# State-space tables of a convolution layer: sums of the last X doubling as identity matmuls on TensorE with ScalarE evictions, Y extension in two wide products, seeds by ScalarE

**Chip, cores, metric.** One core of a Trainium2 chip. The metric is the device time of one execution in microseconds (us). Every ratio below is the mean time of one kernel's fast runs over that of the kernel before's fast runs of the same rounds on the same chip, so it is not quite the ratio of the medians quoted next to it. In the profile lines PE is TensorE, DVE VectorE, ACT ScalarE and SPq SyncE's DMA queue; L311 is a line of the kernel. To evict is to copy a result out of PSUM, where the matmuls here leave theirs.

## The reference

Four layers in a row with residuals: state-space convolution, local attention, and both again. The change touches only the building of the convolution kernel `K` for the first layer, which stays in use for the third.

```python
def _A_ref(u, A_re, A_im, B_re, B_im, C_re, C_im, log_dt, Dskip):   # u: [1, 2048, 512], N = 128 modes
    dt = jnp.exp(log_dt)[:, None]
    logdA = dt * (A_re + 1j * A_im);  dB = dt * Bc
    P = jnp.exp(logdA[:, :, None] * l[None, None, :])               # powers, l = 0..2047
    K = jnp.einsum("dn,dnl,dn->dl", Cc, P, dB).real
    ...                                                             # y = irfft(rfft(u) * rfft(K)), + u * Dskip
x = x + _A_ref(_layernorm(x), ...);  x = x + _B_ref(_layernorm(x), ...)   # twice
```

The kernel factors `l` into two indices: a table X of 32 powers and a table Y of 64 scaled powers, for 64 channels a round, and contracts them over the modes. Eight rounds make the 512 channels.

## The kernel before

The parts that matter, with cuts marked `...`. One round of the tables and their contraction:

```python
def double(self, T, m, lev, hc):                 # entries m..2m-1 from entries 0..m-1 by a complex multiply
    for e0 in range(0, m, HALF):                 # HALF = 8
        ta = self.wk.tile(..., tag="ta");  tb = self.wk.tile(..., tag="tb")       # single scratch tiles
        nc.vector.tensor_tensor(v(ta), src, self.mult(self.MA, lev, hc, mm), ALU.mult)
        nc.vector.tensor_tensor(v(tb), src, self.mult(self.MB, lev, hc, mm), ALU.mult)
        nc.vector.tensor_tensor(T[..., m + e0:m + e0 + mm, :], ta[...], tb[:, ::-1, ...], ALU.add)

def half(hc, between=None):
    Xt, Y, Y2 = T.build(hc)                      # X has two buffers, Y and Y2 one each
    ...
    T.x_part(Xt, hc)                             # seed and four doublings, VectorE
    T.y_base(Y, hc)                              # seed and four doublings, VectorE
    T.y_products(Y, Y2, hc)                      # six products of 2048 elements, VectorE
    r = between() if between is not None else None     # a piece of the convolution
    with tc.high_priority():
        T.contract(Xt, Y, Y2, hc)                # 256 small matmuls into psk, one ScalarE eviction to KTq
    return r
```

The piece of the convolution between two tables has two stages of matmuls, with DMA transposes in between. It is `u_fft` in even rounds (the input) and `k_fft` in odd ones (the kernel `K`). A round on the page is counted from 1 to 8.

```python
def s1(self, rhs_j, n, drow=None):               # first stage
    for jq in range(NJ // 4):                    # four groups of eight matmuls
        ps = self.pst([128, 2, 16, 32])
        ...                                      # 8 matmuls (TensorE)
        self.evac("z", Z[..., jq * 32:(jq + 1) * 32], ps[...])     # one Z eviction (ScalarE), 1.0 us
    return Z

def s2(self, Z, cs, dsts, what):                 # second stage
    zts = self.turns(Z, cs)                      # DMA transposes zt <- Z: they need all four evictions of Z
    ...                                          # 16 matmuls from zt, evictions to xc, W or Kt
```

The scheduler puts the instructions of each engine into one fixed order when the kernel is built. That order is not the order of the source. `high_priority` moves the contraction forward in it.

## Time and profile before

| | before | where it is read |
|---|---|---|
| time | 530.74 us (528.93 to 532.49), 3 runs | times |
| VectorE busy, table stage 62 to 227 us | 153 of 165 us | table of windows (in the prediction) |
| TensorE, ScalarE busy there | 107, 79 us | the same |
| chain that ended last | TensorE 31%, VectorE 28% of the span | page, part 4 |

```profile
195.31 3.78 ACT L298 CAST Z<-psA 128x1024 bf16<-128x1024 f32 x4
202.87 1.01 ACT L688 CAST KTq<-psk 128x1024 bf16<-128x1024 f32 x1 [3.78 <-issue]
207.54 1.01 ACT L298 CAST Kt<-psA 128x1024 bf16<-128x1024 f32 x1 [3.66 <-PE psA L339]
```

In round 4, 26 of the 32 first-stage matmuls (L311) come ahead of the main part of the contraction and 6 behind it. In round 7 all four Z evictions are done before the contraction's eviction KTq. The transposes then run beside the contraction, and the second stage delivers its first tile 4.67 us after KTq (207.54 less 202.87). I call this distance, KTq to the first eviction of the second stage, the **hand-over**.

### The profile page before, as it was taken

How to read it: one execution, taken by the hardware profiler on the slowest of the kernel's cores; microseconds unless marked ns; L12 is line 12 of the kernel's file. 1: busy time of each engine (PE TensorE's matmuls, PEld its weight loads, DVE VectorE, ACT ScalarE, POOL GpSimd, SP SyncE). 2: the span in 40 equal slices, each digit the busy share in tenths (PEclk: the TensorE clock that was granted, in tenths of full speed). 3: DMA queues.
4: the chain of work that ended last, by engine and by line, in shares of the span. 5: the costliest groups of instructions: out<-in, count | busy, mean ns of one | idle time of the engine just before them, and what ended most of it. 6: DMA issues, size and time to landing. Idle time of an engine off the chain costs nothing.

```text
span 524.6 us, 15316 instructions
## 1 busy us (share of the span) xinstructions
PE 383.4 (73%) x6456; PEld 255.8 (49%) x6518; DVE 432.8 (82%) x974; ACT 350.1 (67%) x422; POOL 83.3 (16%) x135
## 2 busy tenths in 40 slices
PE   0200466568469555879898999987799989999996
PEld 0100324346246423656565565655566646666674
DVE  4999999989998998969696566887689999666663
ACT  3999825636265543635676777867788777888872
POOL 0000000000000003051146411134000214911110
PEclk9999998779688967979999899998899999999999
DMA  8301044363446257531437743424397004633532
GB/s 266 144 1 40 1 101 79 65 109 126 105 75 155 44 121 136 191 40 49 164 99 147 153 107 81 72 18 172 73 197 161 1 11 94 126 107 84 101 93 92
DMA packets 104826, 52.52 MB, mean 100 GB/s; under 512 B 86004, under 2 KB 100469, under 8 KB 103477
## 3 DMA queue, kind: packets, MB, share of 16 engines
q1 hardware_dynamic: 103044, 50.88, 42.2%
q8 instruction: 51, 0.84, 0.7%
q10 hardware_dynamic: 1584, 0.39, 0.4%
q0 software_dynamic: 128, 0.26, 0.1%
q14 instruction: 19, 0.15, 0.1%
HBM read 17.96 MB, written 8.13 MB: 50 GB/s over the span
## 4 chain that ended last, share of the span: by engine, by line
PE 31%; DVE 28%; ACT 7%; DMA 5%; issue 5%; POOL 2%; SPq 2%; ACTq 0%; DVEq 0%; POOLq 0%
PE psG L1090 5%; ACT PT L1127 5%; PE psG L1107 4%; PE S L1124 4%; PE O L1143 3%; DVE Ytab L660 3%; DVE Y2tab L662 3%; PE psG L1182 3%; DMA zt<-Z 3%; DVE ln_st_b L216 2%; DVE ta L623 2%; PE S L1182 2%; DVE tb L624 2%; DMA xt<-xq 2%; POOL XU L1262 1%
## 5 line engine op out<-in xcount | busy, mean ns | idle before, releaser
L1127 ACT ACTIVATE PT<-S 128x1824 bf16<-128x1824 f32 x72 | 121.7, 1690 | 35.1 <-PE S L1124 34.6
L1090 PE MATMUL psG<-XU,wqk 128*128 128x512 bf16 x196 | 56.3, 384 | 2.6 <-issue 1.5
L1095 DVE CAST st<-psG 128x512 bf16<-128x512 f32 x56 | 38.5, 688 | 21.0 <-PE psG L1090 20.5
L1143 PEld LDWEIGHTS <-PT 128*128 128x128 bf16 x1152 | 38.9, 96 | 13.0 <-DVE on L1151 1.5
L1107 PE MATMUL psG<-wv,XU 128*128 128x256 bf16 x288 | 40.7, 274 | 0.2 <-DVE st L1095 0.2
L1143 PE MATMUL O<-V,PT 128*128 128x17 bf16 x1120 | 38.9, 171 | 2.0 <-DVE on L1151 1.3
L311 PE MATMUL psA<-X,sb_F 128*128 128x128 bf16 x128 | 13.8, 242 | 36.4 <-ACT X L724 35.2
L311 PEld LDWEIGHTS <-sb_F 128*128 128x128 bf16 x256 | 16.9, 105 | 44.1 <-issue 41.8
L1124 PEld LDWEIGHTS <-KS 32*128 32x128 bf16 x1152 | 20.5, 93 | 28.4 <-issue 23.3
L298 ACT CAST Z<-psA 128x1024 bf16<-128x1024 f32 (+1 forms) x32 | 28.8, 987 | 7.5 <-PE psA L311 7.5
L679 PE MATMUL psk<-Ytab,Xtab 128*32 128x64 bf16 x1024 | 24.0, 209 | 12.0 <-issue 6.8
L1124 PE MATMUL S<-QS,KS 32*128 32x114 bf16 x1152 | 28.1, 211 | 6.1 <-DMA KS<-st 2.8
L336 PE MATMUL psA<-zt,sb_C 128*128 128x512 bf16 x30 | 14.9, 524 | 23.3 <-DMA zt<-Z 23.3
L1151 DVE TENSOR_TENSOR on<-O,rd 128x256 bf16<-128x256 f32 x70 | 29.7, 425 | 2.4
L682 PE MATMUL psk<-Y2tab,Xtab 128*32 128x48 bf16 x1024 | 23.3, 205 | 11.2 <-issue 9.1
L660 DVE TENSOR_TENSOR Ytab<-Ytab,MA 128x2048 bf16<-128x2048 bf16 (+1 forms) x33 | 30.6, 929 | 0.2
L662 DVE TENSOR_TENSOR Y2tab<-Ytab,MB 128x2048 bf16<-128x2048 bf16 (+1 forms) x33 | 30.6, 928 | 0.0
L688 ACT CAST KTq<-psk 128x1024 bf16<-128x1024 f32 (+1 forms) x9 | 8.3, 918 | 33.1 <-issue 32.5
L637 POOL MEMSET Xtab<- 128x64 bf16 x8 | 1.6, 200 | 180.2 <-PE psk L682 161.4
L1107 PEld LDWEIGHTS <-XU 128*128 128x128 bf16 x288 | 25.3, 98 | 6.9 <-issue 0.2
L682 PEld LDWEIGHTS <-Xtab 128*32 128x32 bf16 x1024 | 20.9, 102 | 15.7 <-issue 14.8
L679 PEld LDWEIGHTS <-Xtab 128*32 128x32 bf16 x1024 | 21.4, 107 | 13.0 <-issue 12.2
(252 smaller groups left out, 1060.8 us busy)
## 6 DMA issues: line engine op xcount, KB each, us to landing
kt_scratch<-Kt SPq DMA_DIRECT2D x4, 1024.0 KB, 3.9
Kt<-kt_scratch SPq DMA_DIRECT2D x4, 1024.0 KB, 5.0
QS<-st SPq DMA_DIRECT2D x58, 64.0 KB, 1.9
KS<-st SPq DMA_DIRECT2D x58, 64.0 KB, 1.9
X<-in_A_u_dram SPq DMA_DIRECT2D x4, 512.0 KB, 5.5
out_dram<-X SPq DMA_DIRECT2D x16, 128.0 KB, 1.7
k_scratch<-KTq SPq DMA_DIRECT2D x7, 256.0 KB, 2.5
KT<-k_scratch SPq DMA_DIRECT2D x7, 256.0 KB, 2.8
```

The lines of the kernel that those rows point to most:

```text
L311: nc.tensor.matmul(o, F1[:, j, r, :], rhs_j(j), start=True, stop=not dk)
L660: nc.vector.tensor_tensor(v(Y[:, :, :, q * EYB:(q + 1) * EYB, :]), src, vm(self.mult(self.MA, lev, hc, EYB)), ALU.mult)
L662: nc.vector.tensor_tensor(v(Y2[:, :, :, (q - 1) * EYB:q * EYB, :]), src, vm(self.mult(self.MB, lev, hc, EYB)), ALU.mult)
L679: nc.tensor.matmul(psk[32 * g:32 * g + 32, ds, :], xs, Y[:, m // 2, h, :, t], start=(m == 0), stop=False, skip_group_check=True)
L682: nc.tensor.matmul(psk[32 * g:32 * g + 32, ds, EYB:], xs, Y2[:, 1 - m // 2, h, :, t], start=False, stop=(m == 3), skip_group_check=True)
L1090: nc.tensor.matmul(ps[:], wqk[:, ct, f0:f0 + 128], xnT[:, ct, par, UF + h * 512:UF + h * 512 + 512], start=(ct == 0), stop=(ct == 3))
L1095: eng(t[:], ps[:])
L1107: nc.tensor.matmul(ps[:].rearrange("p h d -> p (h d)"), xnT[:, ct, par, NQ * b + 1:NQ * b + 1 + NK], wv[:, ct, fp * 256:fp * 256 + 256], s ...
L1124: nc.tensor.matmul(S[:, i, sl * NQ:(sl + 1) * NQ], KS[r, e, f2, b * NQ + 1:b * NQ + 1 + NK], QS[r, e, f2, UF + b * NQ:UF + b * NQ + NQ], s ...
L1127: nc.scalar.activation(pt[:, 0:16 * NQ].rearrange("k (i x) -> k i x", i=4), S[:, :, 0:4 * NQ], ACT.Exp, scale=DH ** -0.5)
L1143: nc.tensor.matmul(O[:, x * 8 + i * 2 + e, :], pt[:, c0:c0 + 128], V[:, par * NB + b, (fp * 2 + f2) * 8 + i * 2 + e, :], start=True, stop= ...
L1151: nc.vector.tensor_tensor(on.rearrange("q (h d) -> q h d", d=DH), O[:, :, 0:DH], rd[:].unsqueeze(2).to_broadcast([128, 16, DH]), ALU.mult)
```

## The change

Intent: take work off VectorE, the busiest engine, and give it to TensorE and ScalarE, which stand half idle. The last X doubling becomes two products, one of them straight into X; TensorE adds the two by identity matmuls into PSUM, and ScalarE evicts the sum to X. The three pairs of Y products become two wide ones, which needs a new layout of the tables and multipliers. The seeds go to ScalarE, and three coefficient products move ahead of the ladder. The core of the diff, with cuts marked `...` (the regrouped views of the tables in `contract` and the split products of the last round are left out):

```diff
+    t1, t2 = tmp("t1"), tmp("t2")              # hoisted out of coefs(), ahead of the sine
+    ...
-        nc.scalar.copy(MA[:, i], ...)
+        nc.scalar.copy(MA[:, :, i], ...)         # multipliers: level index inside the channel index
...
+    def double_last(self, X, lev, hc, cv):
+        nc, m = self.nc, EX // 2
+        tb = self.pair()...                      # the one scratch tile "tab", shared with double()
+        nc.vector.tensor_tensor(X[:, :, :, m:, :]..., src, self.mult(self.MA, lev, hc, m), ALU.mult)
+        nc.vector.tensor_tensor(tb..., src, self.mult(self.MB, lev, hc, m), ALU.mult)
+        for c in range(2):
+            ps = cv.pst([128, 2, 512])
+            for q in range(2):
+                hs = slice(16 * q, 16 * q + 16)
+                for k, t in ((0, X[:, c, hs, m:, :]), (1, tb[:, 1 - c, hs])):
+                    nc.tensor.matmul(ps[:, q, :], cv.C["ident"][:], t..., start=(k == 0), stop=(k == 1))
+            nc.scalar.copy(X[:, c, :, m:, :]..., ps[:]...)
...
-        nc.vector.tensor_copy(X[:, :, :, 1, :]..., self.nu[:, hc]...)
+        (nc.vector.tensor_copy if hc == 0 else nc.scalar.copy)(X[:, :, :, 1, :]..., self.nu[:, hc]...)
...
-        for q, lev in ((1, 4), (2, 5), (3, LV48)):      # six products of 2048 elements
+        for lev in ((4,) if whole else (4, 5, 6)):      # whole: two products of 6144
...
             else:
-                T.x_part(Xt, hc)
+                T.x_part(Xt, hc, 4)
                 T.y_base(Y, hc)
+                T.double_last(Xt, 10, hc, cv)
             T.y_products(Y, Y2, hc)
```

More of the change, by code (lines that the diff above doesn't have):

```diff
@@ L518, in ladder @@
     nc.vector.tensor_tensor(ws[:], tb[:], rnd[:], ALU.subtract)
+    t1, t2 = tmp("t1"), tmp("t2")
+    nc.vector.tensor_tensor(t1[:], raw["C_re"][:], raw["B_re"][:], ALU.mult)
+    nc.vector.tensor_tensor(t2[:], raw["C_im"][:], raw["B_im"][:], ALU.mult)
+    nc.vector.tensor_tensor(t1[:], t1[:], t2[:], ALU.subtract)
     sh = tmp("sh")
@@ L540, in coefs @@
     def coefs():
-        t1 = tmp("t1")
-        t2 = tmp("t2")
-        nc.vector.tensor_tensor(t1[:], raw["C_re"][:], raw["B_re"][:], ALU.mult)
-        nc.vector.tensor_tensor(t2[:], raw["C_im"][:], raw["B_im"][:], ALU.mult)
-        nc.vector.tensor_tensor(t1[:], t1[:], t2[:], ALU.subtract)
         nc.vector.tensor_tensor(quad[:, :, 0, :], t1[:], dt_bc, ALU.mult)
@@ L565, in multipliers @@
             return
-        nc.scalar.copy(MA[:, i], src[:, 0].unsqueeze(2).to_broadcast([128, 8, 2, 64]))
+        nc.scalar.copy(MA[:, :, i], src[:, 0].unsqueeze(2).to_broadcast([128, 8, 2, 64]))
         conj = 7 <= i <= 10
-        nc.scalar.activation(MB[:, i, :, 0, :], src[:, 1], ACT.Copy, scale=-1.0 if conj else 1.0)
-        nc.scalar.activation(MB[:, i, :, 1, :], src[:, 1], ACT.Copy, scale=1.0 if conj else -1.0)
+        nc.scalar.activation(MB[:, :, i, 0, :], src[:, 1], ACT.Copy, scale=-1.0 if conj else 1.0)
+        nc.scalar.activation(MB[:, :, i, 1, :], src[:, 1], ACT.Copy, scale=1.0 if conj else -1.0)
     cur = LAM
@@ L608, in mult, with pair @@
     def mult(self, M, lev, hc, n):
-        return (M[:, lev, hc].rearrange("n c (h t) -> n (c h) t", t=2).unsqueeze(2)
+        return (M[:, hc, lev].rearrange("n c (h t) -> n (c h) t", t=2).unsqueeze(2)
                 .to_broadcast([128, 2 * HD, n, 2]))
+    def pair(self):
+        return self.wk.tile([128, 2, 2, HD, HALF * 2], BF, name="tab", tag="tab")
     def double(self, T, m, lev, hc):
@@ L616, in double @@
             mm = min(m, HALF)
-            ta = self.wk.tile([128, 2, HD, HALF * 2], BF, name="ta", tag="ta")
-            tb = self.wk.tile([128, 2, HD, HALF * 2], BF, name="tb", tag="tb")
+            both = self.pair()
+            ta, tb = both[:, 0], both[:, 1]
             def v(t):
-                return t[:].rearrange("n c h (e t) -> n (c h) e t", t=2)[:, :, 0:mm, :]
+                return t.rearrange("n c h (e t) -> n (c h) e t", t=2)[:, :, 0:mm, :]
             src = T[:, :, :, e0:e0 + mm, :].rearrange("n c h e t -> n (c h) e t")
@@ L626, in double, with x_part @@
                                     ta[:, :, :, 0:mm * 2], tb[:, ::-1, :, 0:mm * 2], ALU.add)
+    def double_last(self, X, lev, hc, cv):
+        nc, m = self.nc, EX // 2
+        tb = self.pair()[:].rearrange("n i c h x -> n (i c h x)").rearrange("n (c h e t) -> n c h e t", c=2, e=m, t=2)
+        src = X[:, :, :, 0:m, :].rearrange("n c h e t -> n (c h) e t")
+        nc.vector.tensor_tensor(X[:, :, :, m:, :].rearrange("n c h e t -> n (c h) e t"), src,
+                                self.mult(self.MA, lev, hc, m), ALU.mult)
+        nc.vector.tensor_tensor(tb.rearrange("n c h e t -> n (c h) e t"), src, self.mult(self.MB, lev, hc, m), ALU.mult)
+        for c in range(2):
[3 more added lines that the diff above has]
+                for k, t in ((0, X[:, c, hs, m:, :]), (1, tb[:, 1 - c, hs])):
+                    nc.tensor.matmul(ps[:, q, :], cv.C["ident"][:], t.rearrange("n h e t -> n h (e t)"), start=(k == 0),
+                                     stop=(k == 1))
+            nc.scalar.copy(X[:, c, :, m:, :].rearrange("n h e t -> n h (e t)"),
+                           ps[:].rearrange("n q (h x) -> n (q h) x", x=2 * m))
     def build(self, hc):
-        nc = self.nc
-        Y = self.ty.tile([128, 2, HD, EY, 2], BF, name="Ytab", tag="Ytab")
-        Y2 = self.ty.tile([128, 2, HD, EY - EYB, 2], BF, name="Y2tab", tag="Y2tab")
+        Y = self.ty.tile([128, EY // EYB, 2, HD, EYB, 2], BF, name="Ytab", tag="Ytab")
+        Y2 = self.ty.tile([128, EY // EYB - 1, 2, HD, EYB, 2], BF, name="Y2tab", tag="Y2tab")
         X = self.tx.tile([128, 2, HD, EX, 2], BF, name="Xtab", tag="Xtab")
         return X, Y, Y2
-    def x_part(self, X, hc):
+    def x_part(self, X, hc, top=5):
         nc = self.nc
@@ L638, in x_part @@
         nc.gpsimd.memset(X[:, 1, :, 0, :], 0.0)
-        nc.vector.tensor_copy(X[:, :, :, 1, :].rearrange("n c h t -> n (c h) t"),
-                              self.nu[:, hc].rearrange("n c (h t) -> n (c h) t", t=2))
-        for lev in range(1, 5):
+        (nc.vector.tensor_copy if hc == 0 else nc.scalar.copy)(
+            X[:, :, :, 1, :].rearrange("n c h t -> n (c h) t"),
+            self.nu[:, hc].rearrange("n c (h t) -> n (c h) t", t=2))
+        for lev in range(1, top):
             self.double(X, 1 << lev, 6 + lev, hc)
@@ L644, in y_base @@
     def y_base(self, Y, hc):
-        self.nc.vector.tensor_copy(Y[:, :, :, 0, :].rearrange("n c h t -> n (c h) t"),
-                                   self.cb[:, hc].rearrange("n c (h t) -> n (c h) t", t=2))
+        nc = self.nc
+        (nc.vector.tensor_copy if hc == 0 else nc.scalar.copy)(
+            Y[:, 0, :, :, 0, :].rearrange("n c h t -> n (c h) t"),
+            self.cb[:, hc].rearrange("n c (h t) -> n (c h) t", t=2))
         for lev in range(4):
-            self.double(Y, 1 << lev, lev, hc)
+            self.double(Y[:, 0], 1 << lev, lev, hc)
@@ L650, in y_products @@
     def y_products(self, Y, Y2, hc, h0=0, h1=HD):
-        nc = self.nc
-        if h1 - h0 == HD:
-            views = [(lambda t: t.rearrange("n c h e t -> n (c h) e t"), lambda m: m)]
-        else:
-            views = [(lambda t, c=c: t[:, c, h0:h1], lambda m, c=c: m[:, c * HD + h0:c * HD + h1]) for c in range(2)]
-        for q, lev in ((1, 4), (2, 5), (3, LV48)):
-            for v, vm in views:
-                src = v(Y[:, :, :, 0:EYB, :])
-                nc.vector.tensor_tensor(v(Y[:, :, :, q * EYB:(q + 1) * EYB, :]), src,
-                                        vm(self.mult(self.MA, lev, hc, EYB)), ALU.mult)
-                nc.vector.tensor_tensor(v(Y2[:, :, :, (q - 1) * EYB:q * EYB, :]), src,
-                                        vm(self.mult(self.MB, lev, hc, EYB)), ALU.mult)
+        nc, n = self.nc, EY // EYB - 1
@@ new lines, in y_products @@
+        whole = hc > 0 and h1 - h0 == HD
+        for lev in ((4,) if whole else (4, 5, 6)):
+            k = n if whole else 1
+            for dst, M in ((Y[:, lev - 3:lev - 3 + k], self.MA), (Y2[:, lev - 4:lev - 4 + k], self.MB)):
+                for cs in ((slice(0, 2),) if h1 - h0 == HD else (slice(0, 1), slice(1, 2))):
+                    shape = [128, k, (cs.stop - cs.start) * (h1 - h0), EYB, 2]
+                    nc.vector.tensor_tensor(
+                        dst[:, :, cs, h0:h1].rearrange("n q c h e t -> n q (c h) e t"),
+                        Y[:, 0:1, cs, h0:h1].rearrange("n q c h e t -> n q (c h) e t").to_broadcast(shape),
+                        M[:, hc, lev:lev + k, cs, 2 * h0:2 * h1].rearrange("n q c (h t) -> n q (c h) t", t=2)
+                        .unsqueeze(3).to_broadcast(shape), ALU.mult)
@@ L678, in contract @@
                     if m % 2 == 0:
-                        nc.tensor.matmul(psk[32 * g:32 * g + 32, ds, :], xs, Y[:, m // 2, h, :, t],
+                        nc.tensor.matmul(psk[32 * g:32 * g + 32, ds, :].rearrange("p (q e) -> p q e", e=EYB), xs, Y[:, :, m // 2, h, :, t],
                                          start=(m == 0), stop=False, skip_group_check=True)
                     else:
-                        nc.tensor.matmul(psk[32 * g:32 * g + 32, ds, EYB:], xs, Y2[:, 1 - m // 2, h, :, t],
+                        nc.tensor.matmul(psk[32 * g:32 * g + 32, ds, EYB:].rearrange("p (q e) -> p q e", e=EYB), xs, Y2[:, :, 1 - m // 2, h, :, t],
                                          start=False, stop=(m == 3), skip_group_check=True)
@@ L700, in kernel_and_first_conv @@
         mt = es.enter_context(tc.tile_pool(reuse_waits="tile", name="k_mt", bufs=1))
-        MA = mt.tile([128, 11, 8, 2, 64], BF, name="MA")
-        MB = mt.tile([128, 11, 8, 2, 64], BF, name="MB")
+        MA = mt.tile([128, 8, 11, 2, 64], BF, name="MA")
+        MB = mt.tile([128, 8, 11, 2, 64], BF, name="MB")
         cb = mt.tile([128, 8, 2, 64], BF, name="cb")
@@ L783, in kernel_and_first_conv @@
         Xt, Y, Y2 = T.build(7)
-        T.x_part(Xt, 7)
+        T.x_part(Xt, 7, 4)
         side = T.tx.tile([128, 4096], BF, name="side", tag="Xtab")
@@ L793, in kernel_and_first_conv @@
         T.y_base(Y, 7)
+        T.double_last(Xt, 10, 7, cv)
         T.y_products(Y, Y2, 7, 0, HD // 2)
```

## The prediction

> **What bounds the kernel now.** I read the page first, then windows of stages, then the timelines of VectorE, TensorE and ScalarE side by side. The page's slices show VectorE at nine tenths or more in the first fifteen slices (0 to 200 us), where the state-space tables are built; later TensorE and ScalarE take over. The table of windows divides that into a ladder stage (9 to 62), the table stage (62 to 227) and the rest:
>
> ```profile
> core 0: us, PE busy (x) PEld busy (x) DVE busy (x) ACT busy (x) POOL busy (x), PEclk, DMA share, GB/s
> 9.00:62.00 53.00, 8.39 (x40) 5.38 (x40) 52.12 (x106) 48.17 (x68) 0.00 (x0) 1.00 0.21 77
> 62.00:227.00 165.00, 106.76 (x2526) 71.66 (x2534) 153.24 (x286) 79.33 (x101) 6.10 (x18) 0.83 0.51 107
> 227.00:250.00 23.00, 22.00 (x315) 14.36 (x319) 18.31 (x33) 12.12 (x20) 9.11 (x11) 0.92 0.11 42
> 250.00:524.00 274.00, 246.30 (x3577) 164.37 (x3625) 207.05 (x544) 205.29 (x225) 67.46 (x97) 0.98 0.45 102
> ```
>
> The reader is to see VectorE at 153 of 165 us in the table stage, ScalarE at 79: moving work from one to the other looks free. The change touches only the first 227 us. The groups of VectorE by form give the durations for that stage:
>
> ```profile
> L660 DVE TENSOR_TENSOR Ytab<-Ytab,MA 128x2048 bf16<-128x2048 bf16 x18 | 22.0, 1220 | 0.2
> L623 DVE TENSOR_TENSOR ta<-Xtab,MA 128x1024 bf16<-128x1024 bf16 x21 | 14.5, 692 | 0.7
> L625 DVE TENSOR_TENSOR Xtab<-ta,tb 128x1024 bf16<-128x1024 bf16 x21 | 14.5, 689 | 0.5
> ```
>
> The stage is eight rounds ("halves"): X table by doublings, Y base by doublings, six Y products, then a contraction of 256 small matmuls on TensorE. X has two buffers, Y has **one**. So the next Y seed waits until the contraction has read Y; the next X is built meanwhile. Two timelines show both outcomes, VectorE at one such hand-over and ScalarE's eviction that follows the contraction:
>
> ```profile
> 110.58 0.68 DVE L624 TENSOR_TENSOR tb<-Xtab,MB 128x1024 bf16<-128x1024 bf16 x1
> 113.28 0.24 DVE L645 COPY Ytab<-cb 128x128 bf16<-128x128 bf16 x1 [2.02 <-PE psk L682]
> ```
> ```profile
> 91.19 1.01 ACT L688 CAST KTq<-psk 128x1024 bf16<-128x1024 f32 x1 [5.17 <-issue]
> 113.38 1.01 ACT L688 CAST KTq<-psk 128x1024 bf16<-128x1024 f32 x1 [9.05 <-issue]
> 136.09 1.01 ACT L688 CAST KTq<-psk 128x1024 bf16<-128x1024 f32 x1 [4.25 <-issue]
> 155.07 1.01 ACT L688 CAST KTq<-psk 128x1024 bf16<-128x1024 f32 x1 [3.18 <-issue]
> ```
>
> From the end of the Y products to this eviction I get, round by round, 8.2, 8.3, 9.5, 5.2, 4.0, 5.0 and 4.9 us (products end at 82.87, 103.84, 130.89, 151.04, 177.81 and 197.97 for the second to seventh; round one counts from its last X sum, 61.90). The X part takes 8.1 us (130.81 to 139.15 less two seeds), so it hides a contraction of 5 us and just about one of 8. That X part is what the change shortens.
>
> **What the Trainium skill says.** (1) "VectorE: DVE Perf Modes", section on the perf-mode tier table, gives 1224 ns for a bf16 tensor_tensor over 2048 elements in the 2x mode; this trace has 1219 to 1220, so the mode is on now. (2) "Vector Engine (DVE) Microarchitecture Reference", section 2.1, says a tensor-tensor instruction holds three-dimensional patterns. That explains why the diff moves the level index next to the channel index: the wide product's multiplier then folds to three dimensions, and its innermost pair stays adjacent. I therefore expect 2x to hold for it; no wide form is in this trace. (3) "ScalarE: Activation LUTs", section on what ACT_TABLE_LOAD costs, gives 186 ns plus 0.833 ns per element; for 1024 elements that is 1039 ns against 1.01 us traced, so a 128-element seed is an estimate of 0.29 us. (4) "Runtime: NRT & Kernel Launch", section on instruction fetch mechanics, calls the crossing of a block of 256 instructions mostly hidden. Here TensorE pauses for 2.08 us put to "issue" after 127 contraction matmuls with as many weight loads (87.14). If that is a block edge it is not hidden; the trace doesn't name the cause.
>
> **The change, part by part.** Starts on VectorE follow each other at 1.137 us for 2048 elements and 0.605 for 1024, hence 0.52 ns per element more.
> - Last X doubling, rounds 2 to 8: today two blocks of two products and a sum, 134.99 to 139.14 less the seeds, 3.95 us. After: two products of 2048, 2.27 us. Saved 1.68 x 7 = 11.8 us. Added: 8 matmuls of 512 columns a round (starts in the trace 0.22 us apart at full clock, 0.43 at half: 1.7 to 3.4 us) and two evictions of 1.01 us.
> - Seeds on ScalarE: two starts 0.1 us apart vanish from VectorE, 0.2 x 7 = 1.4 us. X seeds are off the path (two buffers). A Y seed now goes contraction, ScalarE, VectorE: 0.3 us more, and 1.0 more if the eviction goes first, as the contraction's high priority suggests.
> - Wide products, rounds 2 to 7: 6 x 1.137 = 6.82 becomes 2 x (0.605 + 5120 x 0.00052) = 6.53. Saved 0.29 x 6 = 1.7 us. Elements are the same; only start-up is saved.
> - Coefficient products ahead of the sine: VectorE idles 1.92 us before 9.03 waiting for X; three operations of 0.69 us fit there, and the ladder starts so much earlier on both engines. Saved about 1.8 us.
>
> The sum is 16.7 us of VectorE time, 3.1%: a ceiling, 514.
>
> Now the path. With one Y buffer a round is a loop: contraction, seed, Y base (4.9), products (6.53), contraction. The X part hid the contraction; three levels last only 4.15 us. Two orders are possible. **In program order** the last X products (2.27) stand between Y base and products: with a contraction of 5.0 a round is 5.0 + 1.3 + 4.9 + 2.27 + 6.53 = 20.0 us, against 20.15 now (130.89 to 151.04). **If the last X products are pulled forward** into the wait, VectorE is busy to 6.42, but the one scratch tile is then held until TensorE has summed it, behind the contraction: 6.4 + 2.3 (middle of 1.7 and 3.4) + 11.43 = 20.1. With contractions of 8.2 the pulled-forward round is 21.9 against 20.97 now (61.90 to 82.87). So at today's contraction times four rounds break even and three lose about 1 us each: about 3 lost, 1.8 won from the ladder, 532. If all contractions took 5 us, as the later ones do, the first three would win 1 to 2 each, near 525. Which contraction times I shall get depends on where TensorE's stream puts its pauses and transpose waits, so I weigh the cases.
>
> **The rivals.**
> 1. Full relief: the gain is near the ceiling, 515. For it: VectorE is 93% busy and nothing else is near full. Against: the loop on Y just computed. 15%.
> 2. Half relief: hand-overs cost about 1 us a round and contractions shorten, about 523. For it: the tuner moved the work on purpose, and 4 us contractions occur (155.07). 35%.
> 3. A wait takes the place of the work: VectorE waits 2 to 4 us at each hand-over, about 530. For it: the single Y buffer and the single scratch tile. 40%.
> 4. The convolution's chain becomes the bound: in odd rounds TensorE stands 5 us for transposes, then ScalarE runs eight evictions (144.16 to 151.90) right up to the contraction at 151.09; two more evictions and eight matmuls put in there would delay it by 2 us or so. About 537. Against: if the sums run just after the contraction, TensorE is waiting for a transpose anyway. 10%.
> A wide product that fell out of 2x would cost over 3 us more each, 36 us in all; I give that 1 in 100, inside rival 4.
>
> **Range and chances.** The weighted mean is 0.15 x 515 + 0.35 x 523 + 0.40 x 530 + 0.10 x 537 = 526.0; I say 526. The low end 516 is rival 1 almost whole; the high end 535.5 is rival 4 in part. Faster by over 2% needs under 520.1, which asks for rival 1 or the better part of rival 2: 0.20. Slower by over 2% means over 541.4: 0.04. Within: 0.76.
>
> **What would show it right or wrong.** In the new profile: VectorE busy in the table stage down about 15 us; wide products near 3.3 us each; idle of VectorE before the first Y doubling, with the Y seed or a TensorE sum as releaser, some 1 to 4 us a round (none would mean rival 1); the first contraction 1.5 to 2 us earlier; the span after the table stage as before, some 297 us from 227 to the end. I am wrong if rounds shrink by 2 us or more each, which would mean the Y loop has slack I don't see, or if the products take above 4 us, or if the difference appears after the table stage.

## More of the kernel before

The chain is to be held beside the 93% of VectorE. Over the whole span TensorE has a greater share of it than VectorE:

```profile
PE 31%; DVE 28%; ACT 7%; DMA 5%; issue 5%; POOL 2%; SPq 2%; ACTq 0%; DVEq 0%; POOLq 0%
```

This does not hold for the table stage: the largest TensorE lines of this chain (L1090, L1107) are of the attention layers, after 250 us. Cut to 62 to 227 us, the view of the chain names VectorE first (it goes back to 104.34 us only; the line shows its largest parts):

```profile
by line: DVE Ytab L660 9.5%; DVE Y2tab L662 9.1%; DMA zt<-Z 8.4%; issue 7.8%; DVE ta L623 6.7%; DVE tb L624 6.3%; DVE Ytab L625 3.8%; DVE Xtab L625 3.3%; DVE pb L384 3.1%; SPq L270 3.1%; DVE pa L383 3.1%; PE psA L337 1.5%; PE psk L682 1.3%;
```

The VectorE lines among them come to 44.9% of the stretch, those of TensorE to 2.8%. So VectorE was on the longest chain of this stage. How close the next chain comes, such a view does not show.

The view of waits of the kernel before, 62 to 250 us (columns: engine, line, what it waited for, then us in total, times, longest):

```profile
PE psA L336 <- DMA zt<-Z: 23.3, 7, 5.2
PE psA L337 <- DMA zt<-Z: 5.5, 8, 3.2
DVE pa L383 <- ACT Kt L298: 6.7, 6, 3.1
```

TensorE stands 28.8 us (23.3 + 5.5) for the transposes `zt`. The timelines of TensorE in round 4 and of ScalarE in round 7 show where such a wait falls (start, duration, instruction, count, and in brackets the idle time before it and its releaser):

```profile
127.81 1.06 PE L311 MATMUL psA<-X,sb_F 128*128 128x128 bf16 x16
129.96 0.73 PE L311 MATMUL psA<-X,sb_F 128*128 128x128 bf16 x10
135.92 0.82 PE L311 MATMUL psA<-X,sb_F 128*128 128x128 bf16 x6
141.34 1.04 PE L336 MATMUL psA<-zt,sb_C 128*128 128x512 bf16 x2 [4.60 <-DMA zt<-Z]
```

## The result and the profile after

544.34 us (543.24 to 545.58, 4 runs) against 529.84 (525.81 to 532.49, 4 runs): ratio 1.0281 (95%: 1.021 to 1.0353), **slower**. The prediction said 526.0, and 4% for this case.

The table of windows, the same columns as in the prediction, of the kernel after:

```profile
62.00:227.00 165.00, 103.26 (x2281) 64.98 (x2278) 131.23 (x203) 83.97 (x111) 5.63 (x17) 0.84 0.42 89
```

VectorE is relieved: 131 us busy in these 165 instead of 153. But TensorE ran 2281 matmuls in the same window instead of 2526, although it now has more to do: everything happens later. The statistics of the next LayerNorm start at 235.77 before and at 255.32 after (groups `ln_st_b` of VectorE's timeline), 19.6 us later, and the profiled spans differ by 17.7 (542.3 less 524.6). So the loss lies in the table stage and its tail, and 1.9 us come back after it. The chain has turned to TensorE, ScalarE and the DMA. Cut to 62 to 227 us, as above, its largest parts are the transposes `zt` with 15.6%, pauses put to "issue" with 12.6% and ScalarE's Z evictions with 7.7%; the two largest of VectorE have 4.0% each. Over the whole span:

```profile
PE 42%; DVE 19%; ACT 18%; DMA 9%; issue 6%; SPq 3%; POOL 1%; ACTq 0%; DVEq 0%; POOLq 0%
```

The view of waits of the kernel after, the same window as before:

```profile
PE psA L336 <- DMA zt<-Z: 32.9, 7, 6.6
PE psA L337 <- DMA zt<-Z: 9.5, 8, 2.9
DVE pa L383 <- ACT Kt L298: 16.8, 4, 12.1
DVE tab L625 <- PE psA L643: 12.8, 3, 8.0
DVE tab L625 <- ACT Ytab L666: 9.5, 7, 3.6
```

TensorE waits 42.4 us for transposes (28.8 before). VectorE has three waits that are new or grown: for the convolution (16.8), for the scratch tile until the sums have read it (12.8), and for the Y seed (9.5). Round 4 of TensorE, as shown of before:

```profile
129.49 0.81 PE L643 MATMUL psA<-Xtab,sb_ident 128*128 128x512 bf16 x2
130.79 0.44 PE L311 MATMUL psA<-X,sb_F 128*128 128x128 bf16 x5
131.81 0.73 PE L311 MATMUL psA<-X,sb_F 128*128 128x128 bf16 x10
136.96 1.12 PE L311 MATMUL psA<-X,sb_F 128*128 128x128 bf16 x17
144.70 1.04 PE L336 MATMUL psA<-zt,sb_C 128*128 128x512 bf16 x2 [6.62 <-DMA zt<-Z]
```

Now 17 of the 32 first-stage matmuls come behind the contraction, where there were 6. The timeline of ScalarE in round 7 shows what this does:

```profile
209.14 1.96 ACT L645 CAST Xtab<-psA 128x1024 bf16<-128x1024 f32 x2
210.99 1.03 ACT L298 CAST Z<-psA 128x1024 bf16<-128x1024 f32 x1
215.87 1.01 ACT L710 CAST KTq<-psk 128x1024 bf16<-128x1024 f32 x1
216.78 2.84 ACT L298 CAST Z<-psA 128x1024 bf16<-128x1024 f32 x3
225.80 1.01 ACT L298 CAST Kt<-psA 128x1024 bf16<-128x1024 f32 x1 [6.18 <-PE psA L339]
```

One Z eviction comes ahead of KTq and three behind; only then can the transposes start, and no contraction is left to run beside them. The hand-over is 9.93 us (225.80 less 215.87), where it was 4.67. Over rounds 4 to 7 the hand-overs were 8.07, 4.13, 8.06 and 4.67 before, 24.9 us in all; after, they are 10.04, 9.99, 10.81 and 9.93, 40.8 in all. That is 15.8 us more. It is near what was lost (14.5 by the medians), but the match proves nothing: the same sum is 42.1 in r15 below, which lost 1.6%, and 40.9 in r3, which lost nothing. A contraction that ends early also makes a long hand-over.

The rounds, from one KTq to the next, show it more directly. Rounds 2 and 3, whose first stage stands ahead of the contraction after the change too, take 38.5 us instead of 42.8 (KTq of round 1 to that of round 3); rounds 4 to 8 take 133.2 instead of 110.8.

The reason stands in the order of TensorE's instructions, which is fixed when the kernel is built. Counted from the listings of both kernels (first stage, contraction, sum; the number is matmuls), rounds 4 and 5:

```
before  round 4: final 36, first 16, contraction 4, first 10, contraction 252, first 6 | second 16
        round 5: first 26, contraction 4, first 7, contraction 252                     | second 16
after   round 4: final 36, sum 8, first 5, contraction 8, first 10, contraction 248, first 17 | second 16
        round 5: sum 8, first 4, contraction 8, first 11, contraction 248, first 18           | second 16
```

Rounds 6 and 7 repeat this after the change; before it, they leave 1 and 0 behind. (In odd rounds the first stage has 33 matmuls.) The sums are put first, then the contraction, and more than half of the first stage is left behind it: with 15 matmuls ahead of the contraction's main part, only one of the four groups of eight is whole. Why the scheduler weighs it so is not in any trace.

The Trainium skill, "PSUM — Partial Sum Buffer", section on engine and sequencer instructions, says that matmuls "start and complete in program order". This trace agrees: the sums for round 6 have both their products at 167.4 (the last starts at 166.18 and takes 1.23) but run at 186.06, behind the convolution's inverse and final stage. The contraction of round 6 waits with them: both Y tables are ready at 173.94, but it starts at 188.40. In the kernel before they were ready at 177.81, and its main part started at 177.9. So a late second stage delays the next contraction too. Meanwhile VectorE waits for the scratch.

VectorE's order has changed as well. Its products `pa` and `pb` of round 5 stand behind the Y products of round 6: the first starts at 173.86, 1.8 us after its Kt is evicted (172.03); before, it started at 160.24, at once after Kt (160.21). From VectorE's timeline, the first wait of the stage (for an X seed), two products of round 6 (the last of X and the first wide one), the wait for the scratch, and the wait of the last round for the convolution:

```profile
63.87 0.29 DVE L625 TENSOR_TENSOR tab<-Xtab,MA 128x256 bf16<-128x256 bf16 x1 [2.92 <-ACT Xtab L658]
166.18 1.23 DVE L637 TENSOR_TENSOR tab<-Xtab,MB 128x2048 bf16<-128x2048 bf16 x1
167.32 3.35 DVE L681 TENSOR_TENSOR Ytab<-Ytab,MA 128x6144 bf16<-128x6144 bf16 x1
188.06 0.29 DVE L625 TENSOR_TENSOR tab<-Xtab,MA 128x256 bf16<-128x256 bf16 x1 [8.02 <-PE psA L643]
248.72 0.69 DVE L383 TENSOR_TENSOR pa<-xc,Kt 128x1024 bf16<-128x1024 bf16 x1 [12.07 <-ACT Kt L298]
```

### The profile page after: what moved, and what is told of

It reads as the page before. It is cut to its first block, busy times and chain, and to the rows that moved or that the text cites.

```text
span 542.3 us, 15426 instructions
## 1 busy us (share of the span) xinstructions
PE 393.2 (73%) x6509; PEld 259.5 (48%) x6574; DVE 417.5 (77%) x908; ACT 365.8 (67%) x450; POOL 82.7 (15%) x135
## 4 chain that ended last, share of the span: by engine, by line
PE 42%; DVE 19%; ACT 18%; DMA 9%; issue 6%; SPq 3%; POOL 1%; ACTq 0%; DVEq 0%; POOLq 0%
PE psG L1114 6%; DMA zt<-Z 5%; PE psG L1131 5%; PE S L1148 4%; PE O L1167 3%; ACT PT L1151 3%; PE psG L1206 3%; ACT Z L298 2%; DVE ln_st_b L216 2%; PE S L1206 2%; PE psk L701 2%; SPq L270 2%; ACT MA L565 2%; ACT sq L575 2%; PE psk L704 2%
## 5 line engine op out<-in xcount | busy, mean ns | idle before, releaser
L1119 DVE CAST st<-psG 128x512 bf16<-128x512 f32 x56 | 38.5, 687 | 20.4 <-PE psG L1114 19.4
L1167 PEld LDWEIGHTS <-PT 128*128 128x128 bf16 x1152 | 38.9, 96 | 12.8 <-DVE on L1175 1.5
L336 PE MATMUL psA<-zt,sb_C 128*128 128x512 bf16 x30 | 14.4, 522 | 33.3 <-DMA zt<-Z 32.9
L311 PEld LDWEIGHTS <-sb_F 128*128 128x128 bf16 x256 | 16.8, 104 | 43.5 <-issue 40.8
L1148 PE MATMUL S<-QS,KS 32*128 32x114 bf16 x1152 | 28.2, 211 | 5.7 <-DMA KS<-st 2.7
L298 ACT CAST Kt<-psA 128x1024 bf16<-128x1024 f32 x14 | 13.9, 1014 | 24.3 <-PE psA L339 24.2
L681 DVE TENSOR_TENSOR Y2tab<-Ytab,MB 128x512 bf16<-128x512 bf16 (+2 forms) x21 | 28.3, 1369 | 0.0
L681 DVE TENSOR_TENSOR Ytab<-Ytab,MA 128x512 bf16<-128x512 bf16 (+2 forms) x21 | 28.3, 1369 | 0.0
L704 PEld LDWEIGHTS <-Xtab 128*32 128x32 bf16 x1024 | 19.8, 98 | 17.2 <-issue 16.5
L1188 POOL COPY oT<-oS 128x684 bf16<-128x684 bf16 x20 | 15.2, 758 | 76.8 <-DMA oS<-on 76.8
```

The source lines that it names most:

```text
L298: self.nc.scalar.copy(dst, src)
L311: nc.tensor.matmul(o, F1[:, j, r, :], rhs_j(j), start=True, stop=not dk)
L681: nc.vector.tensor_tensor(dst[:, :, cs, h0:h1].rearrange("n q c h e t -> n q (c h) e t"), Y[:, 0:1, cs, h0:h1].rearrange("n q c h e t -> n ...
L704: nc.tensor.matmul(psk[32 * g:32 * g + 32, ds, EYB:].rearrange("p (q e) -> p q e", e=EYB), xs, Y2[:, :, 1 - m // 2, h, :, t], start=False, ...
L1119: eng(t[:], ps[:])
L1148: nc.tensor.matmul(S[:, i, sl * NQ:(sl + 1) * NQ], KS[r, e, f2, b * NQ + 1:b * NQ + 1 + NK], QS[r, e, f2, UF + b * NQ:UF + b * NQ + NQ], s ...
```

## The experiments

**Theory.** The sums make the loss, and mostly not by their own duration: they change TensorE's order, so that first stage, transposes and second stage fall behind the contraction. **Rivals:** the seeds, the wide products or the hoist; the PSUM tiles that the sums take from the convolution; VectorE's wait for the scratch tile; the sums' own time on TensorE and ScalarE. The line numbers of the kernels below are shifted by a few lines.

### Parts of the change

`r1_sum_on_vector`, the last X sums back on VectorE, all else of the change kept:

```diff
-                T.x_part(Xt, hc, 4)
+                T.x_part(Xt, hc)
                 T.y_base(Y, hc)
-                T.double_last(Xt, 10, hc, cv)
```

> The change without its TensorE sums: the last X doubling is made by VectorE again (full X part before the Y base), the wide products, the ScalarE seeds and the earlier coefficient products stay. Theory 1 (with the sums, TensorE's fixed order puts most of the convolution's first stage, and with it the transposes, behind the contraction, so the convolution's chain sets the round): in this build's order only 6 of 32 first-stage matmuls of the even rounds are behind the contraction, as before the change (6), so 525 to 530 us. Theory 2 (the wait of the Y loop: Y seed behind ScalarE, shortened X part): the X part hides the contraction again, 526 to 531 us. Theory 3 (the seeds or the wide products themselves cost the time): 538 us or more.

Measured 529.8 us, ratio 1.0021 (0.9957 to 1.0086): the loss is gone. The ranges of theories 1 and 2 both allow this; r2 parts them.

`r2_only_sums`, the sums alone; seeds, products and coefficients as before:

```diff
-        (nc.vector.tensor_copy if hc == 0 else nc.scalar.copy)(
+        nc.vector.tensor_copy(
-        whole = hc > 0 and h1 - h0 == HD
+        whole = False
```

> Only the TensorE sums of the change: seeds back on VectorE, products in six again, coefficient products in their old place; the two new layouts stay. Theory 1: TensorE's order is that of the changed kernel (17 of 32 first-stage matmuls behind the contraction), so the loss is here whole: 544 to 550 us. Theory 2: without the ScalarE seeds a round loses about 1.3 us less, 532 to 538 us. Theory 3: as before, about 530 us.

Measured 543.82, ratio 1.0284 (1.0227 to 1.0341), the same as the whole change. Its order of TensorE in rounds 4 to 7 is, count by count, that of the whole change. So the sums make the loss, and seeds, wide products and hoist together are worth nothing that these intervals show.

`r3_no_sums`, the sums dropped, so VectorE is relieved and nobody pays (**wrong result**):

```diff
-        for c in range(2):
-            ps = cv.pst([128, 2, 512])
-            ...                                  # identity matmuls and evictions of double_last
```

> Wrong result on purpose: the changed kernel without the eight sum matmuls and the two evictions a round (the upper half of X stays an unsummed product); VectorE's work is that of the changed kernel. It shows what the relief of VectorE is worth when nothing is paid for it. Theory 1: the sums are the cause, directly and by the order; 515 to 524 us. Theory 2 (the loop on the single Y buffer holds the rounds near 20 us whatever VectorE does): 527 to 534 us.

Measured 525.88, ratio 0.9952 (0.9877 to 1.0027). That is between the two ranges: even for nothing the relief is worth about 2.5 us, and the interval includes none at all. The tables do run ahead: the KTq eviction of round 7 starts at 192.13, before at 202.87. But the next one, of round 8, comes 29 us later, at 221.12 (before: 21.3 later, at 224.16). The convolution now ends last. This build also has its own order of TensorE (the contraction of round 6 stands ahead of the whole first stage of that round), so r14 below is the cleaner test of a free relief.

### The order alone

`r4_first_stage_first`, the whole change, with the first stage raised in priority, so that the scheduler puts it ahead of the contraction:

```diff
+        with self.tc.high_priority():            # around the four groups of s1, matmuls and Z evictions
             for jq in range(NJ // 4):
```

> The changed kernel with one thing altered: the convolution's first-stage matmuls and their evictions get the contraction's high priority, and since they come ahead of it in the program they are now all ahead of it in TensorE's order (none of 32 behind, against 17 or 18 in the changed kernel); the sums stay where they are. Theory 1: the transposes start before the contraction again, most of the loss comes back: 526 to 533 us. Theory 2: nothing on VectorE changed, 541 to 547 us. Theory 4 (not the order but the sums' own 8 matmuls and 2 evictions in the convolution's chain, some 3 us a round): a small part comes back, 537 to 541 us.

Measured 526.92, ratio 0.9953 (0.99 to 1.0006): 17 us below the change, with the same work. No first-stage matmul is left behind the contraction (round 5: sum 3, first 9, sum 5, first 15, contraction 4, first 9, contraction 252). The timeline of ScalarE in round 7, and the transpose waits of TensorE in the same window as above:

```profile
207.85 3.83 ACT L299 CAST Kt<-psA 128x1024 bf16<-128x1024 f32 x4 [0.40 <-PE psA L341]
```
```profile
PE psA L338 <- DMA zt<-Z: 6.3, 2, 3.4
PE psA L339 <- DMA zt<-Z: 1.1, 2, 0.9
```

KTq is at 206.45, so the hand-over is 1.40 us, and TensorE waits 7.4 us for transposes instead of 42.4.

`r5_before_split`, the kernel before, with only the order made worse: 16 of the 32 first-stage matmuls pinned behind the contraction in rounds 4 to 7:

```diff
         for jq in range(NJ // 4):
+            with (self.tc.issue_after(behind) if behind is not None else ExitStack()):
                 ps = self.pst([128, 2, 16, 32])
                 ...
+            if jq == 1 and self.mid is not None:
+                behind = self.mid(last.ins)      # the contraction, issued after this group
```

> The kernel before, with nothing changed but TensorE's order in rounds 4 to 7: half of the convolution's first stage (16 of 32 matmuls, and so half of the Z evictions) is pinned behind the contraction, as the changed kernel has it (17 of 32); no sums, no ScalarE seeds, VectorE's instructions unchanged. Theory 1 (the order alone makes the loss): each of those rounds gets 3 to 4 us longer, 538 to 545 us. Theory 4 (the sums' own matmuls and evictions make it): 527 to 532 us, since there are none.

Measured 536.28, ratio 1.0145 (1.0093 to 1.0197): about half of the loss, from order alone, and between the two expected ranges. The sum of hand-overs in rounds 4 to 7 is 36.5 us (24.9 before). The scheduler also moved VectorE's `pa` and `pb` of rounds 5 and 7 back, among or behind the Y products; in r15 and r18 below and in the change it did so too. So "order" means here the whole schedule that goes with TensorE's.

`r6_before_first_stage_first`, the control: r4's edit in the kernel before.

> Control for r4: the kernel before with only the high priority for the first stage. If r4 gained because the high priority is good in itself, this kernel gains as much as r4 did against the changed one, 512 to 518 us. If, as theory 1 has it, r4 only undid what the sums had done to the order, this kernel, whose order was mostly good already (6, 7, 1 and 7 of 32 behind), stays within 1 per cent: 524 to 532 us.

Measured 524.71, ratio 0.9925 (0.9872 to 0.9979). So the kernel before also had a little to gain from the order, and r4 does not beat it.

### What holds r4

`r7_first_stage_first_own_bank`, r4 with the sums in the contraction's PSUM tile instead of the convolution's:

```diff
-            ps = cv.pst([128, 2, 512])
+            ps = self.ps.tile([128, 2, 512], F32, name="psk", tag="psk")
```

> r4 with the sums in the contraction's PSUM tile instead of two of the convolution's three: in the order the first stage is no longer interleaved with the sums. If the sums' hold on the convolution's PSUM buffers is what keeps r4 from the relief, 518 to 524 us; if the Y loop or TensorE's own work is, 525 to 531 us.

Measured 529.48, ratio 1.0012 (0.9941 to 1.0083): nothing won. The PSUM tiles are then hardly what holds r4, but the test is not a clean one: the contraction's tile has one buffer, so the sums now wait for its eviction, and the scheduler placed them differently.

`r8_vector_sum_first_stage_first`, r1 with r4's edit.

> r1 (last X sum on VectorE; wide products, ScalarE seeds, earlier coefficients) with the high priority for the first stage. Beside r4 it says whether the TensorE sums are worth anything once the order is right: theory 1 with a worthwhile relief: r4 is faster by 3 us or more, this one at 528 to 532; if the relief is worth nothing because the rounds are held elsewhere, the two are within 2 us of each other.

Measured 525.17, ratio 0.9936 (0.9863 to 1.0009). With the order right, it makes no visible difference who does the sums.

### The other half of the loss

The next runs look for what stands beside the order. A "pass-through sum" has the sums' eight matmuls and two evictions a round, at their place, but only copies X's upper half onto itself, so VectorE keeps its work and no scratch is held:

```diff
                 T.y_base(Y, hc)
+                T.pass_through(Xt, cv)           # ps = ident @ X upper (each start=True); scalar.copy back to X
```

`r9_split_dummy_sums`: r5 with pass-through sums.

> The kernel before with the split order of r5_before_split (half of the first stage pinned behind the contraction in rounds 4 to 7), and in addition eight identity matmuls and two ScalarE evictions a round that copy the upper half of the finished X table onto itself, so the contraction waits for them. VectorE keeps all its sums and no scratch tile is held. TensorE's order then is that of the changed kernel: sums, 16 of the first stage, contraction, 16 of the first stage. Theory (the order makes half of the loss, and the sums' own 2 to 3 us of TensorE and 2 us of ScalarE a round, in the convolution's chain, make the other half): 541 to 547, ratio near 1.028. Rival (the other half is VectorE's wait for the scratch tile that the sums hold): 534 to 539, like the split alone. Between 539 and 541 neither is shown.

Measured 540.64, ratio 1.0212 (1.014 to 1.0283): in the gap where I had said that neither is shown; it is 0.7 points above r5, and the intervals overlap.

`r10_no_sums_split`: r3 (no sums, **wrong result**) with r5's pinned order.

> The changed kernel without its sums (wrong result on purpose, as r3_no_sums) but with the split order pinned in rounds 4 to 7. VectorE is relieved for free, TensorE and ScalarE carry nothing more, only the order is bad. Theory (the convolution's chain sets the time and the order lengthens it, whatever VectorE does): 532 to 538, 7 to 12 us above r3_no_sums. Rival (VectorE's relief pays for the bad order): 524 to 529.

Measured 531.32, ratio 1.0025 (0.9953 to 1.0096), just below the theory's range. In the bad order VectorE's relief does win something back: 1.2 points against r5 (the intervals just touch).

`r11_first_dummy_sums`: r6 with pass-through sums.

> The kernel before with the first stage ahead (as r6_before_first_stage_first) and the same eight identity matmuls and two evictions a round that copy the upper half of X onto itself. Nothing is relieved. Theory (with the first stage ahead of the contraction the sums fit into TensorE's waits): 524 to 530, at most 4 us above r6. Rival (the sums cost their own time wherever they stand, 4 to 5 us a round in part): 533 or more.

Measured 524.54, ratio 0.9923 (0.985 to 0.9996), as r6 without them: in the good order the sums cost nothing that can be seen.

`r12_own_scratch`: the whole change, with the Y base's doublings using a free part of Y2 as scratch; TensorE's order in rounds 4 to 7 stays the same.

```diff
-            self.double(Y[:, 0], 1 << lev, lev, hc)
+            self.double(Y[:, 0], 1 << lev, lev, hc, Y2[:, 0]...)      # products there, not in "tab"
```

> The changed kernel, but the doublings of the Y base use a part of Y2 (free at that time) for their products, so the tile that the sums hold stops only the next X table. TensorE's order is that of the changed kernel, sums in front and 17 or 18 of the first stage behind the contraction. Theory (the wait for the scratch eats VectorE's relief): VectorE no longer waits for a TensorE sum ahead of a Y doubling, and the time falls to 533 to 539, ratio 1.007 to 1.02. Rival (the order and the sums' lateness for the contraction alone make the loss, the scratch wait lies beside them): 541 to 546.

Measured 545.07, ratio 1.0315 (1.027 to 1.0361): no gain. But the experiment took nothing away. The three waits for the scratch in the change (12.8 us: before 152.16, 188.06 and 210.06) all stand ahead of an **X** doubling, which still uses the scratch. They are in this trace too, 17.6 us in four, with 8.02 again in round 6. So r12 says nothing of the scratch.

`r13_own_scratch_first_stage_first` (r4 with r12's edit) and `r14_no_sums_first_stage_first` (r3, **wrong result**, with r4's edit):

> As r4_first_stage_first (526.9), with the Y base's own scratch as in r12. If the scratch wait is what keeps the relief from showing there: 518 to 523. If the convolution's chain is the bound in that order: 524 to 529, as r4, r6 and r8.

> The changed kernel without its sums (wrong result on purpose), with the first stage ahead: the relief of VectorE for nothing, in the good order. If the convolution's chain is as long as VectorE's, 520 to 526, near r6 (524.7). If VectorE is the bound in that order: 512 to 518.

Measured 525.82, ratio 0.9957 (0.9918 to 0.9996), and 526.92, ratio 0.9985 (0.9953 to 1.0018). In the good order a free relief of VectorE does not move the time (139 us busy in the window 62 to 227 of r4, 138 of r14, 154 of r6). r13 again removes no wait for the scratch (7.3 us in it, 2.5 in r4). r14 came out a microsecond above the range of the theory and 9 above that of its rival.

I then saw that r5 and r10 were milder than the change: 16 matmuls ahead are two whole groups, 15 are one. The next four take this up; r15 and r16 pin 8 ahead and 24 behind (`if jq == 0` in place of `if jq == 1`), r17 gives the whole change the milder 16 and 16.

> The kernel before with only 8 of the 32 first-stage matmuls in front of the contraction in rounds 4 to 7 and 24 behind, so three of the four Z evictions come behind it, as in the changed kernel's trace. Nothing else changed. Theory (the place of the evictions is the whole loss): 541 to 547, ratio near 1.028, against 1.0145 with two evictions behind. Rival (two behind cost as much as three, the rest is the sums): 534 to 539.

> As r10_no_sums_split (531.3; wrong result on purpose) with 8 in front and 24 behind. Theory: 537 to 543, some 6 to 10 us above r10. Rival (the sums themselves make the rest): 529 to 534.

> The changed kernel with 16 first-stage matmuls in front of the contraction in rounds 4 to 7 and 16 behind, instead of 4 or 5 and 10 or 11 and 17 or 18: one Z eviction more in front. Sums, scratch and VectorE's work as in the changed kernel. Theory: 532 to 539, near r10 plus what r9 showed for the sums (3.5). Rival (the sums' lateness makes the rest): 541 to 546.

Measured: r15 538.01, ratio 1.0163 (1.0063 to 1.0264); r16 (**wrong result**) 533.68, ratio 1.008 (0.9995 to 1.0166); r17 537.77, ratio 1.0175 (1.0097 to 1.0254). Without sums, three evictions behind cost hardly more than two (r15 against r5), so the theory that the order is the whole loss is wrong. With the sums, one group more in front wins a whole point back (r17 against the change; these intervals overlap, but r2 and r12, which have the change's order, stand at 1.0284 and 1.0315).

`r18_quarter_dummy_sums`: r15 with pass-through sums. Nothing of the change is in it but the place and the work of the sums, and their hold on two of the convolution's PSUM tiles.

> As r15_before_quarter (1.0163) with the pass-through sums of r9: eight identity matmuls and two evictions a round, in front of the first stage and the contraction, copying X's upper half onto itself. VectorE keeps all its work. Theory (order and sums together make the loss, and work on each other): ratio 1.025 to 1.032, 541 to 546. Rival (they add as in r9, some 0.7% over the order): 1.020 to 1.025, 538 to 541; then something of the change that no run isolates is left, about 1%.

Measured 544.77 (6 runs), ratio 1.031 (1.0276 to 1.0344). That is the whole loss. Its order is near the change's, not equal to it: 24 matmuls of the first stage stand behind, not 17 or 18, but one Z eviction is ahead in both. The timeline of ScalarE in round 7 is that of the change, with VectorE unrelieved and no scratch held:

```profile
210.24 1.96 ACT L642 CAST Xtab<-psA 128x1024 bf16<-128x1024 f32 x2
212.05 1.07 ACT L299 CAST Z<-psA 128x1024 bf16<-128x1024 f32 x1
217.01 1.01 ACT L705 CAST KTq<-psk 128x1024 bf16<-128x1024 f32 x1 [3.89 <-issue]
217.92 2.85 ACT L299 CAST Z<-psA 128x1024 bf16<-128x1024 f32 x3
226.95 1.01 ACT L299 CAST Kt<-psA 128x1024 bf16<-128x1024 f32 x1 [6.18 <-PE psA L344]
```

The pauses of TensorE within the contraction that the view of waits puts to "issue" are not the loss: they come to 18.0 us in the change, to 15.9 before and to 15.1 in r18 (62 to 250 us).

### All together

Ratios to the kernel before, by TensorE's order in rounds 4 to 7 (columns) and by who does the sums (rows):

| | first stage ahead | 16 ahead, 16 behind | 8 (or 15) ahead, the rest behind |
|---|---|---|---|
| VectorE sums, nothing more (before's work) | 0.9925 (r6) | 1.0145 (r5) | 1.0163 (r15) |
| VectorE sums, and pass-through sums on TensorE | 0.9923 (r11) | 1.0212 (r9) | 1.031 (r18) |
| no sums: relief for nothing | 0.9985 (r14) | 1.0025 (r10) | 1.008 (r16) |
| TensorE sums: the change's work | 0.9953 (r4) | 1.0175 (r17) | 1.0281 (the change) |

Each entry has an interval of about half a point to a point either way, so single differences below that mean little. The pattern is this: in the first column the rows differ by 0.6 points, and none is more than 0.8 from the kernel before. From the first column to the last the time grows in every row, clear of the intervals in all but the third; the step from 16 to 8 in the first row is not resolved. In the bad orders the sums' own work costs (0.7 points in r9, 1.5 in r18; only the second is clear of the intervals). That it does so because it stands in the chain of the convolution is argued from the timelines, and the sums' hold on PSUM tiles in this order was not tested apart. The relief of VectorE wins 0.8 to 1.2 (the 0.8 is within the intervals). In the change the relief doesn't show (1.0281 against 1.031). Whether VectorE's wait for the scratch takes it is left open, as r12 did not remove that wait.

No version beats both kernels by a margin worth naming: r6 and r11 are about 0.75% faster than before.

## Why the prediction was wrong

**Right: the costs on VectorE.** The wide products take 3.35 us (said: near 3.3), a seed on ScalarE 0.30 (estimate 0.29, though the formula that the prediction cites is given for ACTIVATE instructions and the seeds are copies). VectorE is relieved in the table stage by 22 us of the fixed window (said: about 15; the window now also holds less of the work, as everything is later, so the 22 are too many). The span after the table stage is within 2 us of that before (287.0 us from the LayerNorm statistics to the end, 288.8 before).

**Right: the relief is not the gain.** The prediction kept 515 at 15%, since the loop on the single Y buffer gives a round of 20 us either way. r3 measured a free relief at 0.5%, not clear of none, and with the first stage ahead it won nothing (r14 at 0.9985, r6 without it at 0.9925). But the reason given was not the one that holds: in r3 the tables do run ahead by 10.7 us (202.87 less 192.13) and the convolution gives it back. Its chain was nearly as long as VectorE's. Neither view of the chain said so: the page's 31% to 28% are of the whole span, and in the stage itself VectorE led. Nor did rounds of 20 us come: after the change rounds 4 to 7 took 28.2, 23.7, 33.3 and 21.5 us.

**Half right: the waits.** VectorE does wait for Y seeds, 9.5 us over seven times, the 1 to 4 us a round that were named. The first contraction starts 1 us earlier (61.09 against 62.05; said 1.5 to 2). It ends no earlier (KTq 70.59 against 70.63), and the next X table waits 2.92 us at 63.87 for its seed on ScalarE; "X seeds are off the path" was wrong for that one.

**The step that failed is rival 4's "Against"**: "if the sums run just after the contraction, TensorE is waiting for a transpose anyway", and with it the 10% and the 537. The rival was the right one: "The convolution's chain becomes the bound". But its size was taken as the sums' own time, "two more evictions and eight matmuls put in there would delay it by 2 us or so", with everything else of TensorE's stream in its place. The runs show three things in place of that. First, the sums reorder the stream: the first stage goes behind the contraction, so the transpose wait that was to hide the sums grows from 28.8 to 42.4 us, and the hand-overs of four rounds by 15.8 us. The order alone costs 1.45 to 1.6% (r5, r15). Second, in that order the sums' own work, with the PSUM tiles that it holds, nearly doubles the loss (r18: 3.1%, r15: 1.6%). Third, undoing the order alone takes the loss away, with all the work left in (r4: 0.9953). The prediction asked what each instruction costs and which waits end last. It never asked where the scheduler would put the new instructions, though it noted that "which contraction times I shall get depends on where TensorE's stream puts its pauses and transpose waits". That doubt belonged in the range, to the slow side.

**Slips without weight for the result.** Of the distances to the eviction, the 8.2 of round one runs to the Y seed at 70.08; to the eviction at 70.63 it is 8.7. The middle of 1.7 and 3.4 is 2.55, not 2.3. Of the first fifteen slices of VectorE, three are below nine tenths (the first has 4, the ninth and thirteenth 8).

## What to carry to other kernels

An engine with idle time in its busy shares is not free when it works through one fixed order: what is put into it can push something else behind a long block, and the price is that of what was pushed. After moving work to another engine, count the order of its instructions before and after around the longest block, and look at whether the transfers that block used to hide still start ahead of it. And when two chains are nearly equally long, relieving the busiest engine wins little (here 0.5% at most, not clear of noise), while a bad order of the other chain loses more (1.5% alone, 3% with the added work in it); try the free relief, with a wrong result, before building the real one.

## What the Trainium skill lacked or had wrong

- "Perfetto Trace Analysis", section on identifying the most-contended engine, takes the engine with the highest occupancy as the one to optimize first. Here that was VectorE, 153 of 165 us in the stage. Relieving it for nothing gave a ratio of 0.9952 (r3), and 0.9985 with the first stage ahead (r14; 0.9925 without the relief, r6), while a change of TensorE's order alone moved the time by 17 us (r4 against the change). That section lacks the case of two chains nearly equally long, and a word on the order in an engine's queue.
- No page that I read tells what added matmuls do to the scheduled order of those around them. The runs show 26 of 32 first-stage matmuls ahead of the contraction's main part before and 15 after in round 4, and a hand-over of 9.93 us instead of 4.67 in round 7.
- "Runtime: NRT & Kernel Launch", on instruction fetch, as the prediction quotes it: TensorE pauses of about 2 us put to "issue" stand within the contraction in both kernels (before the change 2.37 us ahead of 134.99, after it 2.18 ahead of 136.19). The trace doesn't name their cause, so whether the page is wrong here stays open.
